# Cosine attention and a quick-GELU layer: the issue order of all engines taken from an earliest-due-first plan, and the softmax denominators of three head pairs stored together

## The chip, the core and the metric

The kernel runs on one core of a Trainium2 chip. Its engines work at the same time, each through its own instructions in the order in which the program gives them: TensorE (PE) multiplies matrices, VectorE (DVE), ScalarE (ACT) and GpSimd (POOL) work on elements, and SyncE (SP) issues most transfers (DMA); POOL issues those of the weights. An instruction waits until what it reads is there and the buffer that it writes is free, and what stands behind it on its engine waits too. The metric is the device time of one execution in microseconds.

## The reference, cut to what matters

```
q_n = q / (norm(q) + 1e-06);  k_n = k / (norm(k) + 1e-06)     # 8 batches, 12 heads, 448 rows, 64 columns
attn = softmax(q_n @ k_n.T / tau)                             # tau = 0.1
x = (attn @ v), heads side by side                            # 3584 x 768
h = x @ w_in                                                  # 768 x 2048
out = (h * (1 / (1 + exp(-1.702 * h)))) @ w_out               # 3584 x 768, float32
```

## The kernel before

The work is cut into 48 **head pairs** x (6 of each batch b). A pair goes through these steps: the loads of q, k and v (`load_qk`, `load_v`, SP, 224 KB each); the squares (`square`, ACT) and their sums (`reduce`, DVE); the inverse norms of a group of pairs (`norm`, ten small DVE instructions); q and k times the norms (`scale`, POOL) and v cast to fp16 (`cast_v`, POOL); the transposes (`transposes`, PE, 8 small matmuls into `tps`, which DVE copies to `qkT`); four chunks of scores (`scores`, PE, into `sp`) and their exponentials (`exp`, ACT); and two attention products (`attend`, PE, into `avp`, one for each head of the pair), which DVE moves to `av`. A row of `av` holds the softmax denominators. Three pairs make a **group** g: its denominators go to DRAM (`den_out`), come back spread over the partitions (`den_in`), are inverted (`den_rcp`, DVE), stored, and come back spread to all partitions as `rcb`; then `normalise` (DVE) makes `xT` from `av` and `rcb`.

When the six `xT` of a batch are there, the layer of that batch can run: 16 blocks of `mm1` (6 matmuls each, line 278, then a tanh on ACT and `gT` on DVE) and then 6 or 8 blocks of `mm2` (16 matmuls each, line 318, then `ost` on ACT and the store of the output).

The order is written out by hand. A loop takes two steps s to a pair. In each step it issues two chunks of scores with their exponentials and one attention product of the pair before, and then the jobs that `at(s, ...)` has put down for that step, half of them and then the other half. Between these `fill` takes matmuls from the queue of the layer, until the share of a step is used up; the share is the work that is left over the steps that are left. Every job stands at a fixed step: the loads at `sq_step` less five, `normalise` five or three steps after the last pair of its group, the first layer block of a batch two steps behind that. The weights are asked for by POOL, `w_in` in four pieces at steps 3, 5, 7 and 9, `w_out` at steps 11 to 17.

Buffers that matter: six for each of q and k, four for v, three `sq`, three `qks`, two `qkT`, two `sp`, eight exponentials, six `av` (one for each pair), three `mm` in PSUM, and one in PSUM that `tps` and `avp` share.

## Time and profile before

| | us |
|---|---|
| median of 3 runs (556.71 to 561.02) | 559.64 |
| the profiled execution, its own time | 559.58 |
| its span, from the first instruction to the last | 557.8 |
| PE busy in the span | 474.8 |
| ACT busy | 310.5 |
| DVE busy | 303.2 |
| POOL busy | 140.7 |

The profile has a page and views that ask the trace. The page cuts the span into 40 equal slices (a digit is the busy share in tenths). Stretches give the busy time of each engine between two times. The waits say for which instruction an engine stood idle, how long in total, how many times, and the longest. The timeline lists instructions by their start, with the idle time before them in brackets and what ended it. All times are in us from the first instruction, durations called "mean" are in ns.

### The profile page before, as it was taken

The page shows a single profiled execution, that of the slowest core. Times are in us where ns is not written, and L with a number is a line of the kernel's source. Part 1 is how long each engine was busy: PE and PEld are TensorE (multiplying, and loading weights), DVE is VectorE, ACT ScalarE, POOL GpSimd, SP SyncE. Part 2 cuts the span into 40 slices and gives each one's busy share as a digit, 9 for nine tenths or more (in the row PEclk, how much of TensorE's full clock was granted, in tenths as well). Part 3 has the DMA queues.
Part 4 walks back from the last instruction along what each step waited for, and adds up shares of the span by engine and source line. Part 5 has one row for each costly group of instructions (what it writes and reads, how often), then busy time and mean ns, then how long its engine had stood idle before and what let it go on. Part 6 is the DMA issues. An engine that isn't in the chain of part 4 may idle for free.

```text
span 557.8 us, 7958 instructions
## 1 busy us (share of the span) xinstructions
PE 474.8 (85%) x2816; PEld 236.2 (42%) x2816; DVE 303.2 (54%) x677; ACT 310.5 (56%) x473; POOL 140.7 (25%) x205
## 2 busy tenths in 40 slices
PE   0665617699989999999889998999799999996996
PEld 0222202244544554445344554455344554452553
DVE  6456355667267645675476636764676525532510
ACT  3745707277557655775757656765667445621421
POOL 2370624320403232322323050323232320000000
PEclk9997758699999999999999999999899999997999
DMA  8568979621531436132613343143502220002012
GB/s 237 159 124 179 177 171 175 142 84 58 146 100 51 124 108 181 49 93 80 181 50 110 96 130 116 52 121 108 152 18 60 64 82 29 26 30 82 1 28 86
DMA packets 55431, 56.61 MB, mean 101 GB/s; under 512 B 8064, under 2 KB 51936, under 8 KB 55392
## 3 DMA queue, kind: packets, MB, share of 16 engines
q1 hardware_dynamic: 50144, 49.82, 31.8%
q0 software_dynamic: 5248, 6.29, 7.0%
q8 instruction: 22, 0.36, 0.3%
q14 instruction: 17, 0.14, 0.1%
HBM read 51.20 MB, written 11.18 MB: 112 GB/s over the span
## 4 chain that ended last, share of the span: by engine, by line
PE 65%; DVE 18%; DMA 10%; issue 2%; ACT 2%; SPq 2%; DVEq 0%; ACTq 0%
PE mm L318 23%; PE mm L278 21%; PE avp L213 12%; PE sp L191 8%; DVE xT L263 4%; DVE av L221 3%; DVE n L114 3%; DMA rcp<-rcg 3%; DMA rcb<-rcp 3%; DVE qkT L180 2%; DMA v<-in_v_dram 2%; DVE gT L288 2%; PE tps L174 2%; ACT th L287 2%; DMA q<-in_q_dram 1%
## 5 line engine op out<-in xcount | busy, mean ns | idle before, releaser
L203 ACT ACTIVATE expT<-sp 112x896 f16<-112x896 f32 x192 | 170.3, 914 | 80.6 <-PE sp L191 79.7
L278 PE MATMUL mm<-xT,w_in 128*128 128x448 f16 x768 | 170.2, 362 | 18.6 <-DVE xT L263 18.6
L318 PE MATMUL mm<-w_out,gT 128*128 128x384 f16 x896 | 160.8, 327 | 0.0
L221 DVE TENSOR_SCALAR av<-avp 65x448 f16<-65x448 f32 x96 | 59.5, 620 | 115.1 <-PE avp L213 111.5
L288 DVE SCALAR_TENSOR_TENSOR gT<-th,mm 128x448 f16<-128x448 f16 x128 | 79.0, 620 | 78.0 <-ACT th L287 76.1
L287 ACT ACTIVATE th<-mm 128x448 f16<-128x448 f32 x128 | 69.5, 543 | 88.3 <-PE mm L278 86.7
L318 PEld LDWEIGHTS <-gT 128*128 128x128 f16 x896 | 84.0, 98 | 65.6 <-issue 11.5
L278 PEld LDWEIGHTS <-w_in 128*128 128x128 f16 x768 | 72.4, 99 | 86.8 <-issue 29.5
L156 POOL TENSOR_TENSOR qks<-k,y 112x512 f16<-112x512 f32 x48 | 50.5, 1053 | 188.4 <-DVE y L147 170.8
L213 PE MATMUL avp<-expT,vt 112*128 112x448 f16 x384 | 97.3, 379 | 0.0
L191 PE MATMUL sp<-qkT 64*112 64x448 f16 x384 | 64.2, 411 | 28.6 <-DVE qkT L180 25.5
L167 POOL CAST vt<-v 112x256 f16<-112x256 f32 x96 | 37.2, 401 | 130.8 <-PE avp L213 124.7
L114 DVE TENSOR_REDUCE n<-sq 112x8 f32<-112x512 f32 x96 | 63.9, 676 | 6.0 <-ACT sq L108 5.4
L326 ACT ACTIVATE ost<-mm 128x384 f32<-128x384 f32 x56 | 27.4, 490 | 65.9 <-PE mm L318 63.1
L174 PE MATMUL tps<-ident,qks 112*128 112x112 f16 x384 | 28.9, 223 | 31.1 <-DVE av L221 21.1
L213 PEld LDWEIGHTS <-vt 112*128 112x128 f16 x384 | 36.8, 102 | 43.8 <-issue 16.9
L156 POOL TENSOR_TENSOR qks<-q,y 112x512 f16<-112x512 f32 x47 | 49.2, 1048 | 0.0
L174 PEld LDWEIGHTS <-qks 112*128 112x128 f16 x384 | 25.3, 103 | 54.0 <-issue 39.3
L191 PEld LDWEIGHTS <-qkT 64*112 64x112 f16 x384 | 19.5, 135 | 66.3 <-DVE qkT L180 38.8
L263 DVE TENSOR_TENSOR xT<-av,rcb 64x448 f16<-64x448 f16 x96 | 39.3, 409 | 14.7 <-DMA rcb<-rcp 13.1
L108 ACT ACTIVATE sq<-k 112x512 f32<-112x512 f32 x48 | 30.3, 632 | 6.7 <-DMA k<-in_k_dram 5.2
L180 DVE COPY qkT<-tps 128x896 f16<-128x896 f16 x48 | 29.6, 618 | 5.7 <-PE tps L174 5.4
(23 smaller groups left out, 87.4 us busy)
## 6 DMA issues: line engine op xcount, KB each, us to landing
q<-in_q_dram SPq DMA_DIRECT2D x48, 224.0 KB
k<-in_k_dram SPq DMA_DIRECT2D x48, 224.0 KB
v<-in_v_dram SPq DMA_DIRECT2D x48, 224.0 KB
rcb<-rcp SPq DMA_DIRECT2D x32, 168.0 KB
w_in<-in_moe_w_in_dram POOLq DMA_DIRECT2D x4, 768.0 KB, 10.7
w_out<-in_moe_w_out_dram POOLq DMA_DIRECT2D x4, 768.0 KB, 10.1
out_dram<-ost SPq DMA_DIRECT2D x7, 336.0 KB
out_dram<-ost SPq DMA_DIRECT2D x8, 288.0 KB
```

The costliest lines, as they stand in the source:

```text
L114: nc.vector.tensor_reduce(out=n2s[grp][:, x - grp[0], ti], in_=sqs.pop((x, ti)), axis=AX.X, op=ALU.add,)
L156: (eng or nc.gpsimd).tensor_tensor(out=qkss[x][:, ti].rearrange("p c j d -> p j c d"), in0=src, in1=rss[x][:, ti, :, :, None].to_broadcast ...
L174: nc.tensor.transpose(out=tps[:, ti, c * P : (c + 1) * P], in_=qks[:, ti, c].rearrange("p j d -> p (j d)"), identity=ident[:P, :P],)
L191: nc.tensor.matmul(out=sp[:, j, :S], lhsT=qkT[64 * j : 64 * (j + 1), 1, c * P : (c + 1) * P], rhs=qkT[64 * j : 64 * (j + 1), 0, :], start= ...
L203: nc.scalar.activation(out=e, in_=sps.pop((x, c))[:, :, :S], func=AF.Exp, scale=inv_tau, **kw)
L213: nc.tensor.matmul(out=ps, lhsT=vts[x % 4][:, c, j], rhs=exps[x, c][:, j], start=(c == 0), stop=(c == C - 1),)
L221: nc.vector.tensor_scalar(out=avs[x][:n, j], in0=ps[:n], scalar1=AV_SCALE, scalar2=None, op0=ALU.mult)
L263: nc.vector.tensor_tensor(out=xT[r], in0=av[r, j], in1=rcbs[x // GRP][r, x % GRP], op=ALU.mult)
L278: nc.tensor.matmul(out=ps[:, :S], lhsT=w_in_sb[:, kk, 128 * m : 128 * (m + 1)], rhs=xTs[b, kk], start=(kk == 0), stop=(kk == KT1 - 1),)
L287: nc.scalar.activation(out=th, in_=ps[:, :S], func=AF.Tanh, scale=0.851)
L288: nc.vector.scalar_tensor_tensor(out=gT[:, m], in0=th, scalar=1.0, in1=ps[:, :S], op0=ALU.add, op1=ALU.mult,)
L318: nc.tensor.matmul(out=ps[:, :NW], lhsT=gT[:, kk, 128 * t : 128 * (t + 1)], rhs=w_out_sb[:, kk, cols], start=(kk == 0), stop=(kk == KT2 - 1),)
```

## The change

A class `Plan` replaces the loop over steps, `at`, `fill` and the streams. Every operation is put down with its engine, a duration, a due step, what it comes after, and the buffers that it takes and gives back as counted slots. `order` then runs a clock over that model: an engine that is idle takes, of what is ready and finds its slots free, the operation that is due first. Transfers move one after the other in the queue of their issuer at 270 KB per us (half of that while the other issuer's queue is busy) and land 1.9 us later. The instructions are issued in the order in which the operations start in the model; the engines themselves still wait for data and buffers, not for the model's times.

Due steps are two to a pair as before; the layer of a batch is due from five steps after its last pair on (`LAG`). Some operations are cut apart so that each stands on one engine: the copy out of PSUM from the matmuls, the tanh and the gate from `mm1`, `norm` in two halves, a `mm2` block in four parts of four matmuls. The k load of a pair stands ahead of its q load.

`av` is one tile for three pairs, in two buffers, where each pair had one of six. So the denominators of a group leave in two stores (one for each j, three rows of 448) where there were six of one row: 32 stores in place of 96. No matmul, activation or load is added or removed.

```diff
-MM1_NS = 189
-MM2_NS = 163
...
+SEM_US = 0.1
+SWITCH_US = 0.12
+DMA_US = 1.9
+DMA_BYTES_PER_US = 270e3
...
+class Plan:
...
+    def order(self):
...
+        while len(out) < len(ops):
+            for e in idle:
+                held = []
+                while idle[e] <= now and ready[e]:
+                    due, i = heapq.heappop(ready[e])
+                    _, us, _, emit, _, takes, _, nbytes, rows = ops[i]
+                    if any(self.free[s] < k for s, k in takes):
+                        held.append((due, i))
+                        continue
+                    for s, k in takes:
+                        self.free[s] -= k
+                    out.append((now, i, emit))
+                    if e == "PE" and rows != mode:
+                        mode = rows
+                        us += SWITCH_US
+                    idle[e] = end = now + us
+                    if nbytes is not None:
+                        share = 2 if any(t > end for q, t in dma.items() if q != e) else 1
+                        dma[e] = max(dma.get(e, 0.0), end) + share * nbytes / DMA_BYTES_PER_US
+                        end = dma[e] + DMA_US
+                    heapq.heappush(events, (idle[e], i, True))
+                    heapq.heappush(events, (end + SEM_US, i, False))
...
+            now = events[0][0]
+            while events and events[0][0] <= now:
+                _, i, own = heapq.heappop(events)
+                if not own:
+                    for s, k in ops[i][6]:
+                        self.free[s] += k
...
-    p_av = pool("p_av", 6)
+    p_av = pool("p_av", 2)
...
-            avs[x] = p_av.tile([128, 2, S], FP16, name="av")
...
+    def attended(x, j):
+        if j == 0 and x % GRP == 0:
+            av = p_av.tile([128, GRP, 2, S], FP16, name="av")
+            for i in range(GRP):
+                avs[x + i] = av[:, i]
+            avgs[x // GRP] = av
...
-    def den_out(x, j):
...
-        nc.sync.dma_start(out=dens[x // GRP][r : r + 1, :], in_=avs[x][row : row + 1, j])
...
+    def den_out(g, j):
+        if j == 0:
+            dens[g] = dram.tile([2, GRP, S], FP16, name="den")
...
+        nc.sync.dma_start(out=dens[g][j : j + 1], in_=avgs[g][row : row + 1, :, j])
...
+    plan = Plan(
+        dict(q=6, k=6, v=4, sq=3, qks=3, vt=4, qkT=2, sp=2, a=1, exp=8, av=6)
+        | dict(x=2 * HP, mm=3, th=3, g=1, ost=3)
+    )
...
+    LAG = 5
...
+            add(("sq", ti, x), "ACT", 0.53, early - 2 + ti * 0.1, partial(square, x, ti),
+                after=[("load", nm, x)], takes=[("sq", 1)])
...
+        add(("tp", x), "PE", 0.45, s - 1, partial(transposes, x),
+            after=[("scale", 0, x), ("scale", 1, x)], takes=[("a", 1), ("qkT", 1)], frees=[("qks", 2)])
...
+        add(("x", x), "DVE", 0.75, 2 * (g + 1) * GRP + 3, partial(normalise, x), after=rin,
+            takes=[("x", 1)], frees=[("av", 1)])
...
+            add(("mm1", b, m), "PE", 1.134, due, partial(mm1, b, m), after=after,
+                takes=[("mm", 1)], frees=[("x", HP * (m == KT2 - 1))])
...
-        at(3 + 2 * i, load_w_in, i)
-        at(11 + 2 * i, load_w_out, i)
...
+        add(("w_in", i), "POOL", 1.0, 3 + 2 * i, partial(load_w_in, i), after=[("cast", i)], nbytes=1.57e6)
+        add(("w_out", i), "POOL", 1.0, 11 + 2 * i, partial(load_w_out, i), after=[("w_in", 3)], nbytes=1.57e6)
...
-    for s in range(min(later), max(max(later), 2 * NPAIR + 2) + 1):
...
-            scores(x, half)
...
+    for _, _, emit in plan.order():
+        emit()
```

Three places show how instructions move. The first is POOL at the start of the program: `CAST vt` is the cast of v (x2 for the two heads), `qks` the scaling, `DMA w_in` a piece of the weights. Before:

```order
L156 TENSOR_TENSOR qks<-k_122,y_187 112x2x4x64
L167 CAST vt_116<-v_132 112x4x64 x2
L156 TENSOR_TENSOR qks<-k_126,y_213 112x2x4x64
L156 TENSOR_TENSOR qks<-q_124,y_213 112x2x4x64
L167 CAST vt_117<-v_138 112x4x64 x2
L156 TENSOR_TENSOR qks<-k_130,y_213 112x2x4x64
L156 TENSOR_TENSOR qks<-q_128,y_213 112x2x4x64
L167 CAST vt_118<-v_144 112x4x64 x2
L156 TENSOR_TENSOR qks<-k_136,y_341 112x2x4x64
L156 TENSOR_TENSOR qks<-q_134,y_341 112x2x4x64
L167 CAST vt_119<-v_150 112x4x64 x2
L357 DMA w_in<-in_moe_w_in_dram 128x6x512
```

And with the change:

```order
L238 CAST vt_116<-v_148 112x4x64 x2
L420 DMA w_in<-in_moe_w_in_dram 128x6x512
L227 TENSOR_TENSOR qks<-k_140,y_171 112x2x4x64
L238 CAST vt_117<-v_156 112x4x64 x2
L420 DMA w_in<-in_moe_w_in_dram 128x6x512
L238 CAST vt_118<-v_167 112x4x64 x2
L420 DMA w_in<-in_moe_w_in_dram 128x6x512
L227 TENSOR_TENSOR qks<-k_144,y_215 112x2x4x64
L227 TENSOR_TENSOR qks<-q_146,y_215 112x2x4x64
L227 TENSOR_TENSOR qks<-k_150,y_215 112x2x4x64
L227 TENSOR_TENSOR qks<-q_152,y_215 112x2x4x64
L238 CAST vt_119<-v_189 112x4x64 x2
```

The first three pieces of `w_in` now stand behind the casts of pairs 0, 1 and 2, and the fourth follows the last row shown; before, the first piece stood behind the cast of pair 3. The four pieces of `w_out` now stand together behind the scaling of pair 10's k; before, one stood behind each of the casts of pairs 7 to 10.

The second place is SP around the denominators of the first group of pairs (0 to 2). `den` is the store of denominators, `dnm` the load that brings them back, `rcp` the store of their inverses, `rcb` the load that spreads these. Before, from the fifth of the group's six stores on:

```order
L233 DMA den_313<-av_460 1x448
L101 DMA v32_474<-in_v_dram 112x2x256
L93 DMA q32_476<-in_q_dram 112x2x256
L93 DMA k32_478<-in_k_dram 112x2x256
L233 DMA den_313<-av_460 1x448
L240 DMA dnm_514<-den_313 112x24
L93 DMA q32_521<-in_q_dram 112x2x256
L93 DMA k32_523<-in_k_dram 112x2x256
L233 DMA den_547<-av_536 1x448
L101 DMA v32_549<-in_v_dram 112x2x256
L247 DMA rcp_584<-rcg_582 112x24
L250 DMA rcb_586<-rcp_584 64x3x448 x2
```

With the change, from the rows behind that group's two stores on:

```order
L164 DMA k32_536<-in_k_dram 112x2x256
L164 DMA q32_541<-in_q_dram 112x2x256
L317 DMA dnm_573<-den_483 112x24
L164 DMA v32_585<-in_v_dram 112x2x256
L164 DMA k32_596<-in_k_dram 112x2x256
L164 DMA q32_599<-in_q_dram 112x2x256
L327 DMA rcp_648<-rcg_635 112x24
L164 DMA v32_668<-in_v_dram 112x2x256
L164 DMA k32_677<-in_k_dram 112x2x256
L164 DMA q32_681<-in_q_dram 112x2x256
L310 DMA den_689<-av_578 3x1x448 x2
L332 DMA rcb_709<-rcp_648 64x1344 x2
```

The stores of single pairs are gone from between the loads. Ahead of the first `den` stand 28 loads (22 before), ahead of the first group's `rcb` 37 (35 before), and ahead of the second group's 43 (44 before). The `rcb` of the first group stands behind the `den` of the second.

The third place is DVE where the first `xT` are made. `av_691` is the output of pair 5, `av_357` the tile of pairs 0 to 2, `av_810` that of pairs 6 to 8; `n2_3` are sums of squares; the first `qkT` of each excerpt is pair 6's before and pair 8's now. Before:

```order
L180 COPY qkT_669<-tps_660 128x896
L221 TENSOR_SCALAR av_691<-avp_692 65x448
L114 TENSOR_REDUCE n2_3_632<-sq_653 112x8
L114 TENSOR_REDUCE n2_3_632<-sq_655 112x8
L263 TENSOR_TENSOR xT0_704<-av_302,rcb_586 64x448 x2
L263 TENSOR_TENSOR xT1_707<-av_381,rcb_586 64x448 x2
L221 TENSOR_SCALAR av_691<-avp_723 128x448
```

With the change:

```order
L254 COPY qkT_760<-tps_729 128x896
L177 TENSOR_REDUCE n2_3_793<-sq_782 112x8
L177 TENSOR_REDUCE n2_3_793<-sq_791 112x8
L343 TENSOR_TENSOR xT0_800<-av_357,rcb_709 64x448 x2
L343 TENSOR_TENSOR xT1_803<-av_357,rcb_709 64x448 x2
L343 TENSOR_TENSOR xT2_807<-av_357,rcb_709 64x448 x2
L299 TENSOR_SCALAR av_810<-avp_769 65x448
L299 TENSOR_SCALAR av_810<-avp_813 128x448
```

Before, the first two pairs' `xT` stood between the two halves of pair 5's `av`, and pair 7's `qkT` behind them. Now the `qkT` of pairs 7 and 8 stand ahead of all three pairs' `xT`, and the two halves of pair 6's `av` behind.

## Rows read from the trace of the kernel before

**Rows 1.** The page: busy us (share of the span) and instructions; then PE's busy tenths in 40 slices.

```profile
PE 474.8 (85%) x2816; PEld 236.2 (42%) x2816; DVE 303.2 (54%) x677; ACT 310.5 (56%) x473; POOL 140.7 (25%) x205
...
PE   0665617699989999999889998999799999996996
```

**Rows 2.** Stretches: length, busy (instructions) by engine, PE clock, DMA share, GB/s.

```profile
10.00:98.00 88.00, 49.08 (x233) 19.19 (x234) 47.49 (x115) 46.80 (x66) 37.57 (x55) 0.83 0.80 170
...
106.00:506.00 400.00, 381.24 (x2352) 193.66 (x2351) 230.62 (x495) 244.84 (x375) 98.00 (x140) 0.99 0.31 89
```

**Rows 3.** Waits of PE from 0 to 98: us in total, times, longest.

```profile
PE sp L191 <- DVE qkT L180: 20.6, 10, 5.1
PE tps L174 <- DVE av L221: 16.6, 8, 9.3
PE tps L174 <- POOL qks L156: 10.1, 1, 10.1
```

**Rows 4.** Timeline, 60 to 106: start, us, engine, line, out<-in, count, [idle before <-releaser].

```profile
60.71 0.55 PE L174 MATMUL tps<-ident,qks 112*128 112x112 f16 x8 [0.71 <-DVE av L221]
...
65.76 0.63 ACT L108 ACTIVATE sq<-k 112x512 f32<-112x512 f32 x1 [0.65 <-DVE n L114]
...
66.30 1.70 ACT L203 ACTIVATE expT<-sp 112x896 f16<-112x896 f32 x2
...
71.85 0.38 DVE L263 TENSOR_TENSOR xT<-av,rcb 64x448 f16<-64x448 f16 x1 [5.53 <-DMA rcb<-rcp]
...
74.21 1.19 DVE L263 TENSOR_TENSOR xT<-av,rcb 64x448 f16<-64x448 f16 x3 [1.97 <-DMA rcb<-rcp]
...
75.43 0.62 DVE L221 TENSOR_SCALAR av<-avp 128x448 f16<-128x448 f32 x1
76.08 1.28 DVE L114 TENSOR_REDUCE n<-sq 112x8 f32<-112x512 f32 x2
76.10 0.90 PE L174 MATMUL tps<-ident,qks 112*128 112x112 f16 x8 [9.26 <-DVE av L221]
...
78.02 0.24 SPq L233 DMA_DIRECT2D den<-av  x1
...
80.10 1.03 POOL L156 TENSOR_TENSOR qks<-k,y 112x512 f16<-112x512 f32 x1 [13.28 <-DVE y L147]
...
105.17 0.53 PE L278 MATMUL mm<-xT,w_in 128*128 128x448 f16 x1 [1.53 <-DVE xT L263]
```

**Rows 5.** DMA queues: packets, MB, share of 16 engines; first 0 to 14, then 28 to 60.

```profile
q1 hardware_dynamic: 3456, 3.31, 86.8%
...
q0 software_dynamic: 2383, 2.39, 47.7%
q1 hardware_dynamic: 2538, 2.30, 25.6%
```

**Rows 6.** The weights' issue: ns min/median/max, first and last start.

```profile
L357 POOL DMA_DIRECT2D w_in<-in_moe_w_in_dram x4: 882/883/1009, 31.6 to 57.1; - x4
```

**Rows 7.** Waits of PE from 106 to 506.

```profile
PE mm L278 <- DVE xT L263: 8.0, 8, 1.7
PE sp L191 <- DVE qkT L180: 4.9, 14, 0.8
PE tps L174 <- DVE av L221: 4.4, 7, 0.7
PE sp L191 <- ACT expT L203: 0.8, 2, 0.4
```

**Rows 8.** Waits of PE from 506 to 514.

```profile
PE mm L278 <- DVE xT L263: 5.3, 3, 4.7
```

**Rows 9.** Timeline around the last batch's layer.

```profile
495.99 3.58 PE L318 MATMUL mm<-w_out,gT 128*128 128x384 f16 x21
...
500.17 5.85 PE L318 MATMUL mm<-w_out,gT 128*128 128x384 f16 x35
...
510.81 2.06 DVE L263 TENSOR_TENSOR xT<-av,rcb 64x448 f16<-64x448 f16 x5 [0.72 <-DMA rcb<-rcp]
```

More of the change, by code (lines that the diff above doesn't have):

```diff
@@ L298, in store, with mm1, tanh @@
-    def store(b2, t, ost, cols):
+    gts, mms, ths, osts = {}, {}, {}, {}
+    def mm1(b, m):
+        ps = mms[b, m] = ps_m.tile([128, 512], FP32, name="mm")
+        for kk in range(KT1):
+            nc.tensor.matmul(
+                out=ps[:, :S],
+                lhsT=w_in_sb[:, kk, 128 * m : 128 * (m + 1)],
+                rhs=xTs[b, kk],
+                start=(kk == 0),
+                stop=(kk == KT1 - 1),
+            )
+    def tanh(b, m):
+        ths[b, m] = p_th.tile([128, S], FP16, name="th")
+        nc.scalar.activation(
+            out=ths[b, m], in_=mms[b, m][:, :S], func=AF.Tanh, scale=0.851
+        )
@@ new lines, in gate, with mm2 @@
+    def gate(b, m):
+        if b % 2 == 0 and m == 0:
+            gts[b // 2] = p_g.tile([128, KT2, 2 * S], FP16, name="gT")
+        nc.vector.scalar_tensor_tensor(
+            out=gts[b // 2][:, m, (b % 2) * S : (b % 2 + 1) * S],
+            in0=ths.pop((b, m)),
+            scalar=1.0,
+            in1=mms.pop((b, m))[:, :S],
+            op0=ALU.add,
+            op1=ALU.mult,
+        )
+    def mm2(b2, t, n, part):
+        if part == 0:
+            mms[b2, t, n] = ps_m.tile([128, 512], FP32, name="mm")
+        for kk in range(4 * part, 4 * part + 4):
+            nc.tensor.matmul(
+                out=mms[b2, t, n][:, :NW],
+                lhsT=gts[b2][:, kk, 128 * t : 128 * (t + 1)],
+                rhs=w_out_sb[:, kk, NW * n : NW * (n + 1)],
+                start=(kk == 0),
+                stop=(kk == KT2 - 1),
+            )
@@ new lines @@
+        if x == grp[0]:
+            reds = [("red", ti, y) for y in grp for ti in range(2)]
+            add(("norm", 0, grp), "DVE", 0.9, early, partial(norm_a, grp), after=reds)
+            add(("norm", 1, grp), "DVE", 1.3, early, partial(norm_b, grp), after=[("norm", 0, grp)])
+        add(("load", "v", x), "SP", 0.5, s - 9, partial(load, x, v32, v, "v32"),
+            after=[("s", x - 4, 0)] if x >= 4 else [], takes=[("v", 1)], nbytes=PAIR_BYTES)
+        add(("cast", x), "POOL", 0.75, s - 1, partial(cast_v, x), after=[("load", "v", x)],
+            takes=[("vt", 1)], frees=[("v", 1)])
@@ new lines @@
+        add(("tp", x), "PE", 0.45, s - 1, partial(transposes, x),
+            after=[("scale", 0, x), ("scale", 1, x)], takes=[("a", 1), ("qkT", 1)], frees=[("qks", 2)])
+        add(("qkT", x), "DVE", 0.53, s - 1, partial(transposed, x), after=[("tp", x)],
+            frees=[("a", 1)])
+        for c in range(C):
+            add(("s", x, c), "PE", 0.19, s + c // 2, partial(scores, x, c), after=[("qkT", x)],
+                takes=[("sp", 1)], frees=[("qkT", int(c == C - 1))], rows=64)
+            add(("exp", x, c), "ACT", 0.83, s + c // 2 + 0.1, partial(exp, x, c),
+                after=[("s", x, c)], takes=[("exp", 1)], frees=[("sp", 1)])
@@ new lines @@
+        for j in range(2):
+            es = [("exp", x, c) for c in range(C)] + [("cast", x)]
+            if j == 1:
+                es.append(("av", x, 0))
+            add(("at", x, j), "PE", 0.757, s + 2 + j, partial(attend, x, j), after=es,
+                takes=[("a", 1)], frees=[("exp", 4 * j), ("vt", j)])
+            add(("av", x, j), "DVE", 0.54, s + 2 + j, partial(attended, x, j), after=[("at", x, j)],
+                takes=[("av", 1 - j)], frees=[("a", 1)])
+            if x % GRP == GRP - 1:
+                add(("den", g, j), "SP", 0.45, s + 2 + j, partial(den_out, g, j),
+                    after=[("av", y, j) for y in range(x - GRP + 1, x + 1)], nbytes=3e3)
```

332 lines of the change are left out of this document (155 added, 177 removed).

## The prediction

> **What bounds the kernel now.** I read the page first. PE is the busiest engine, 474.8 of 557.8 us, and its slices fall into three parts: a thin start of about 100 us, a dense middle, and a dip near the end [rows 1]. So I asked for the stretches and for PE's waits in each.
>
> In the middle, 106 to 506, PE is busy for 381.24 of 400 us [rows 2]: it is the bound there, and no order can give back more than the 18.8 us that it stands idle. The waits name 18.1 of these: for `xT` 8.0, for `qkT` 4.9, for `av` 4.4, for exponentials 0.8 [rows 7].
>
> In the start nothing is dense. From 10 to 98 PE is busy for 49 of 88 us, the transfers take 0.80 of their engines, and ACT, DVE and POOL about half of their time [rows 2]. PE waits 47.3 us there, for `qkT` (20.6), `av` (16.6) and `qks` (10.1) [rows 3]. The timeline shows how the longest comes about. DVE stands at an `xT` that waits for `rcb`, 5.53 us and again 1.97; the second half of pair 5's `av`, whose product is long done, stands behind it and starts at 75.43; so `tps`, which needs that buffer of PSUM, starts at 76.10 after 9.26 us. The last denominator store of batch 0 goes at 78.02, and the sixth matmul of the first layer block, which needs the last `xT` of that batch, at 105.17 [rows 4]. From there on PE has work at all times, so **the start is worth what that matmul moves**, since in both orders nine and a half pairs of attention stand ahead of it.
>
> Near the end PE waits 5.3 us for the last batch's `xT` [rows 8]. After that everything depends on one batch's layer, which the change leaves alone.
>
> The profiled execution took 559.58 us, 1.8 over its span and the same as the median of 559.64. The sum is made against 559.6.
>
> **Term 1, the start.** The transfers first. Alone, 3.31 MB of loads took 86.8% of 14 us, and in the mixed stretch ten loads (2.30 MB) took 25.6% of 32 us, so a load costs 0.82 us of all 16 engines. There 2.39 MB of weights (three pieces of 0.786 MB) took 47.7%, so a piece costs 5.0 us [rows 5]. The transposes of pair 6 were the first that the old order held up for long; they started at 60.71 [rows 4]. They need the norms of pairs 6 to 8, so the 25th load in SP's new order, and by then all four pieces of `w_in` have been asked for as well. That is 25 x 0.82 + 4 x 5.0 = 40.5 us of transfers: 40.5 us if the engines never rest, 50.6 at the 0.80 of now. From the sums of squares (76.08) to the scaling (80.10, and 1.03 for each of k and q) take 6.1 us more [rows 4]. So these transposes start between 47 and 57; I take 52.
>
> The second products of pair 5 come one pair's step later. ACT sets that step: four exponentials (1.70 for two) and two squares (0.63 each) are 4.7 us [rows 4]. Then comes the chain from `den` to the first block. It took 27.2 us at the start of this kernel (78.02 to 105.17) [rows 4]. Near the end, with nothing ahead in the queue, it took from the last product (matmuls go on at 500.17) to the end of the last `xT` at 512.87, that is 12.7 us [rows 9]. The new order sends one store for three pairs, without waits between the loads, but three loads still stand between each two of its steps, so I take 23, nearer the upper end. 52 + 4.7 + 23 is 80 for the matmul that is at 105.17 now: **minus 25**. The bounds: 57 + 4.7 + 27.2 = 89, minus 16. On the other side the chain ends at 64, but ACT's four pairs (6 to 9, 18.8 us behind 47, and the scores of a tenth) do not: 70, minus 35.
>
> By the Trainium skill's page "DMA: Bandwidth & Descriptors", section "Queues, rings and completion order", each transfer engine takes turns between the queues that have work, packet by packet. By that rule the loads keep half of the engines while `w_in` is under way, and the sum would be 11 us lower (505; the second rival works it out from rows). The trace agrees in the mixed stretch as far as bytes go, 2.30 and 2.39 MB [rows 5].
>
> What the start pays for this: POOL does a cast and an issue of 0.88 us [rows 6] ahead of the first scaling, so the first transposes come up to 1.7 us later. I cost that at nothing, since the transposes of pair 6 wait for transfers; without that cover it is 1.7. The two more copies `qkT` ahead of the first `xT` on DVE are work that PE can use while `rcb` is under way; that is where the 9.26 us went. Next to be late are pair 6's two `av`, which stand behind all three pairs' `xT`; behind them wait `rcg` of the second group and the `qkT` of pair 9. That lies inside the 23 us. `w_out` is asked for in one go behind the scaling of pair 10's k; its four pieces are 20 us of transfers, and the first `mm2` stands behind all 16 blocks of a batch's `mm1`, so I cost them at nothing; if they came 5 us late, it is 5.
>
> **Term 2, the middle.** Of 18.1 us I expect 14 back. The waits for `xT` (8.0 in eight) come from `normalise` standing at a fixed step, right at the first block that needs it. Now the block is issued only when the plan has the six `xT`, and half a block of `mm2` and a pair of score chunks more stand between the last product of a batch and its first layer block. The waits for `av` (4.4) are those of `tps` behind a product: between them stood one block of `mm1`, and now mostly a pair of score chunks and one block. The `qkT` waits shrink for the same reason: a product stands between transposes and scores. The bounds: nothing (each wait replaced by another of its size) and 18.8 (all idle time of the stretch). New waits can come where a product now follows the transposes after a single block of `mm1` and needs the PSUM buffer that the copy `qkT` must empty first; I leave 4 us for these. **Minus 14.** The 64 stores fewer (0.24 us of SP each) are off PE's path.
>
> **Term 3, the end.** Behind the last product stand 64 matmuls of `mm2` where 32 stood. 21 of them take 3.58 us [rows 9], so 32 more cover 5.4 us of a wait of 5.3 [rows 8]. The chain itself is no shorter than its transfers. I take **minus 4.6**; the bounds are 0 (the chain grows as much) and 5.3.
>
> **The sum:** 559.6 - 25 - 14 - 4.6 = **516**.
>
> **Rivals.**
> - *The weights hold the loads back.* `w_in` was asked for at 31.6 to 57.1 [rows 6], and now three pieces stand among the first POOL rows. If the loads get the worse share, pair 6 starts no earlier than 60.7 and the chain keeps its 27.2: 60.7 + 4.7 + 27.2 = 92.6, minus 12.6. The time is 528. For it: 0.80 is already high. Against: 20.5 us of loads and 20 of weights fit into 60 with room.
> - *The loads keep half.* In the mixed stretch the two queues moved the same bytes. If the first seven loads run alone (5.7 us) and the next 18 at half pace (29.5), the norms follow at 35 with `w_in` unfinished, and pair 6 starts at 41: 41 + 4.7 + 23 = 69, minus 36. The time is 505. Against: `w_in` itself took more than its half there, 47.7% to 25.6% [rows 5].
> - *The middle swaps its waits.* In a fixed line an operation that the plan has too early stops its engine; then term 2 is nothing, 530. For it: each of ACT and DVE is busy for 0.6 of the middle, in order. Against: the new order keeps the blocks' buffers and the spacing.
> - *Nothing is gained:* a new wait of the start's size, 20 us, takes the place of the old ones, and the middle swaps its waits: 559.6 - 5 = 555.
> - *Slower: the tile of three pairs.* The first `av` of group g+2 must now wait for all three `xT` of group g, where one sufficed, and `av`, `qkT` and gates queue behind it on DVE. This is the 9.26 us of rows 4, if it came back at each group. It must eat 43.6 us and 5.6 more; over the 14 groups with a predecessor that is 3.5 us a group. At 4 us it is 572. Against it: in the middle a group of three pairs lasts 30 us (400 us hold 13.3 groups) and the chain 12.7 to 27.2, and no wait for `av` there exceeds 0.7 [rows 7].
>
> **How the numbers follow.** The forecast 0.48 (508 to 527), the weights first 0.15, loads at half 0.10, the middle's waits swapped 0.15, nothing gained 0.07, slower 0.05. The range from 502 to 538 holds the first four, less a little at each edge, and goes no further. A measurement of this kernel can tell about 1%, 5.6 us, from no change: faster 0.88, within it 0.07, slower 0.05.
>
> **What would show it.** Term 1: the sixth matmul of the first layer block near 80, pair 6's transposes near 52, `w_in` issued between about 8 and 25. Term 2: waits for `xT` in the middle under 2 us in all, PE busy over 0.97. Term 3: the wait ahead of the last batch's layer under 1.5 us. It is wrong if the first layer block starts after 95, if PE waits for `av` or `qkT` by more than 10 us in the middle, or if a new wait of DVE for `rcb` appears at every group.

## The result, and the profile after

The changed kernel takes **514.22 us** (median of 4 runs, 512.71 to 516.54) where the kernel before takes 560.33 (median of 4): a ratio of 0.9187, 95% interval 0.9123 to 0.9251. The forecast was 516, between 502 and 538. The profiled execution took 516.54 us with a span of 514.7, against 559.58 and 557.8: 43.0 us less, where the sum of the prediction had 43.6. It is the slowest of the four runs of the changed kernel; by the medians the gain is 46.1 us. The stretches below are those of the profiled executions.

The total is nearly the one forecast, but its parts are not. Here is the span of both kernels cut at the same three places: the sixth matmul of the first layer block, the first matmul of the last batch's layer, and the sixth matmul there. First the kernel before (length, then busy time and instructions of PE, PEld, DVE, ACT, POOL, PE clock, DMA share, GB/s; PEld is the loading of weights into PE, PE clock the granted share of full speed):

```profile
0.00:105.17 105.17, 50.84 (x237) 19.65 (x238) 60.34 (x160) 52.34 (x73) 42.74 (x65) 0.83 0.80 176
105.17:505.86 400.69, 381.92 (x2356) 194.16 (x2356) 230.62 (x495) 245.10 (x375) 98.00 (x140) 0.99 0.31 89
505.86:512.92 7.06, 1.79 (x6) 0.50 (x5) 2.31 (x6) 0.49 (x1) 0.00 (x0) 0.81 0.34 104
512.92:557.80 44.88, 40.22 (x219) 21.91 (x218) 9.94 (x16) 12.61 (x24) 0.00 (x0) 0.95 0.13 36
```

And the changed kernel:

```profile
0.00:90.78 90.78, 56.24 (x255) 22.61 (x256) 60.80 (x162) 55.14 (x75) 42.38 (x65) 0.76 0.89 202
90.78:466.29 375.51, 373.53 (x2339) 192.54 (x2337) 232.37 (x494) 241.72 (x373) 100.57 (x140) 0.99 0.34 96
466.29:471.10 4.81, 1.61 (x6) 0.49 (x5) 2.32 (x6) 0.49 (x1) 0.00 (x0) 0.89 0.51 151
471.10:514.75 43.65, 39.30 (x219) 21.66 (x218) 9.94 (x16) 12.63 (x24) 0.00 (x0) 0.97 0.13 37
```

The start shrank by 14.4 us, the middle by 25.2, the stretch with the wait near the end by 2.25, and the last layer by 1.2. The prediction had 25, 14 and 4.6 for the first three. It took the same work to stand ahead of the first cut in both orders, but in the changed kernel 18 more matmuls do (255 for 237), worth 1.7 us at the rate of the middle (8 transposes of 49 ns, 6 score matmuls of 97, 4 product matmuls of 189), so on equal work it gained 16.1 and the middle 23.5.

The page's slices, to be set against [rows 1] (PE's busy share and granted clock in tenths, 40 slices of 12.9 us):

```profile
PE   0677767998999999999999999999999999997996
...
PEclk9986656899999999999999999999999999998999
```

The dense part now begins at the eighth slice and has no thin digit before the end. PE's waits in it, to be set against [rows 7]:

```profile
PE tps L245 <- DVE av L299: 0.8, 1, 0.8
PE avp L282 <- DVE qkT L254: 0.7, 1, 0.7
```

1.5 us instead of 18.1, and none for `xT`; DVE waits for `rcb` 0.4 us ahead of the last group. What the prediction wanted to see of term 2 is there: PE is busy for 373.53 of 375.51 us.

**The start.** The `w_in` pieces are issued at 8.98, 12.17, 13.79 and 19.49 (31.6 to 57.1 in [rows 6]). Pair 6's transposes start at 52.09, as forecast (52). The timeline shows what they stood behind (start, us, engine, line, operation; in brackets the idle time before and what ended it):

```profile
42.00 0.21 DVE L218 TENSOR_TENSOR y<-y,t 112x48 f32<-112x48 f32 x1
...
42.34 1.04 POOL L227 TENSOR_TENSOR qks<-k,y 112x512 f16<-112x512 f32 x1 [3.93 <-issue]
...
43.34 1.04 POOL L227 TENSOR_TENSOR qks<-q,y 112x512 f16<-112x512 f32 x1
...
47.20 1.65 PE L282 MATMUL avp<-expT,vt 112*128 112x448 f16 x4 [0.71 <-DVE av L299]
...
49.70 1.68 PE L282 MATMUL avp<-expT,vt 112*128 112x448 f16 x4
...
51.42 0.62 DVE L299 TENSOR_SCALAR av<-avp 128x448 f16<-128x448 f32 x1 [1.32 <-PE avp L282]
...
52.09 0.91 PE L245 MATMUL tps<-ident,qks 112*128 112x112 f16 x8 [0.71 <-DVE av L299]
```

The norms are out at 42.2 and k and q of pair 6 are scaled by 44.4. What stands between this and 52 is a chain of PE and DVE over the one PSUM buffer that `avp` and `tps` share: a product, its `av`, the next product, each round 2.4 us, because four matmuls of a product take 1.65 us there where they take 0.92 at 27.39 or in the middle. The first layer block comes 10.8 us later than forecast:

```profile
66.30 2.38 DVE L343 TENSOR_TENSOR xT<-av,rcb 64x448 f16<-64x448 f16 x6
...
71.13 0.62 DVE L299 TENSOR_SCALAR av<-avp 128x448 f16<-128x448 f32 x1 [1.74 <-PE avp L282]
...
72.39 0.29 DVE L322 RECIPROCAL rcg<-dnm 112x24 f16<-112x24 f16 x1
...
77.61 1.12 SPq L332 DMA_DIRECT2D rcb<-rcp  x2
...
85.40 0.62 DVE L254 COPY qkT<-tps 128x896 f16<-128x896 f16 x1
...
85.94 3.10 DVE L343 TENSOR_TENSOR xT<-av,rcb 64x448 f16<-64x448 f16 x6
...
88.94 2.42 PE L354 MATMUL mm<-xT,w_in 128*128 128x448 f16 x6
```

`rcg` of the second group, whose data were asked for at 61.82, runs at 72.39 behind the three pairs' `xT` and two halves of `av`, though the last packet of that load had moved at 65.0; `xT` of pairs 3 to 5 run at 85.94 without waiting for anything, right behind the `qkT` of pair 10.

**The end**, to be set against [rows 8, 9]:

```profile
460.22 0.30 DVE L322 RECIPROCAL rcg<-dnm 112x24 f16<-112x24 f16 x1 [3.50 <-DMA dnm<-den]
...
461.80 0.79 SPq L412 DMA_DIRECT2D out_dram<-ost  x2
462.69 0.37 SPq L327 DMA_DIRECT2D rcp<-rcg  x1
...
464.89 1.14 SPq L332 DMA_DIRECT2D rcb<-rcp  x2
...
468.57 2.48 DVE L343 TENSOR_TENSOR xT<-av,rcb 64x448 f16<-64x448 f16 x6 [8.05 <-DMA rcb<-rcp]
469.43 0.35 PE L354 MATMUL mm<-xT,w_in 128*128 128x448 f16 x1 [2.41 <-DVE xT L343]
```

64 matmuls now stand behind the last product (35 before, [rows 9]), but the chain to the last `xT` (471.05) takes 15.0 us from the last product's end (456.05), where it took 12.5 (500.33 to 512.87). `rcp` was issued at 462.69, though `rcg` had ended at 460.52: on SP two stores of the output stood ahead of it, waiting for their `ost` at 461.29. PE waited 3.2 us.

### The profile page after: what moved, and what is told of

The parts are those of the page before. It is cut to its first block, busy times and chain, and to the rows that moved or that the text cites. A ratio compares the mean times of both kernels' runs of the same rounds, so it can differ in the third digit from the quotient of the medians.

```text
span 514.7 us, 7833 instructions
## 1 busy us (share of the span) xinstructions
PE 470.7 (91%) x2816; PEld 237.3 (46%) x2816; DVE 305.4 (59%) x677; ACT 310.0 (60%) x473; POOL 143.0 (28%) x205
## 4 chain that ended last, share of the span: by engine, by line
PE 75%; DVE 9%; DMA 1%; ACT 1%; issue 1%; SPq 0%; DVEq 0%; ACTq 0%
PE mm L384 27%; PE mm L354 25%; PE avp L282 12%; PE sp L263 7%; PE tps L245 3%; DVE xT L343 3%; DVE gT L371 2%; DVE av L299 1%; DVE qkT L254 1%; DVE n L177 1%; DMA rcb<-rcp 1%; DMA rcp<-rcg 0%; ACT expT L274 0%; DVE t L203 0%; DVE t L206 0%
## 5 line engine op out<-in xcount | busy, mean ns | idle before, releaser
L274 ACT ACTIVATE expT<-sp 112x896 f16<-112x896 f32 x192 | 166.1, 915 | 68.5 <-PE sp L263 62.6
L354 PE MATMUL mm<-xT,w_in 128*128 128x448 f16 x768 | 159.9, 359 | 3.2 <-DVE xT L343 3.2
L384 PE MATMUL mm<-w_out,gT 128*128 128x384 f16 x896 | 155.4, 326 | 0.0
L238 POOL CAST vt<-v 112x256 f16<-112x256 f32 x96 | 40.6, 425 | 268.5 <-PE avp L282 256.1
L384 PEld LDWEIGHTS <-gT 128*128 128x128 f16 x896 | 83.8, 98 | 63.7 <-issue 12.5
L282 PE MATMUL avp<-expT,vt 112*128 112x448 f16 x384 | 98.9, 384 | 12.6 <-DVE qkT L254 6.2
L282 PEld LDWEIGHTS <-vt 112*128 112x128 f16 x384 | 38.6, 103 | 56.0 <-issue 29.4
L227 POOL TENSOR_TENSOR qks<-k,y 112x512 f16<-112x512 f32 x48 | 50.0, 1043 | 12.5 <-issue 7.0
L343 DVE TENSOR_TENSOR xT<-av,rcb 64x448 f16<-64x448 f16 x96 | 38.8, 404 | 10.1 <-DMA rcb<-rcp 8.5
```

Of the source, the lines that this page charges most:

```text
L227: (eng or nc.gpsimd).tensor_tensor(out=qkss[x][:, ti].rearrange("p c j d -> p j c d"), in0=src, in1=rss[x][:, ti, :, :, None].to_broadcast ...
L274: nc.scalar.activation(out=e, in_=sps.pop((x, c))[:, :, :S], func=AF.Exp, scale=inv_tau, **kw)
L282: nc.tensor.matmul(out=ps, lhsT=vts[x % 4][:, c, j], rhs=exps[x, c][:, j], start=(c == 0), stop=(c == C - 1),)
L343: nc.vector.tensor_tensor(out=xT[r], in0=av[r, j], in1=rcbs[x // GRP][r, x % GRP], op=ALU.mult)
L354: nc.tensor.matmul(out=ps[:, :S], lhsT=w_in_sb[:, kk, 128 * m : 128 * (m + 1)], rhs=xTs[b, kk], start=(kk == 0), stop=(kk == KT1 - 1),)
L384: nc.tensor.matmul(out=mms[b2, t, n][:, :NW], lhsT=gts[b2][:, kk, 128 * t : 128 * (t + 1)], rhs=w_out_sb[:, kk, NW * n : NW * (n + 1)], st ...
```

## The experiments

All of these ran with the kernel before beside them; a ratio is that to the kernel before. The last four columns are the same four stretches of each profiled execution, by the start of the matmuls.

| kernel | median us | ratio (95%) | start | middle | wait | last layer |
|---|---|---|---|---|---|---|
| before | 560.33 | | 105.2 | 400.7 | 7.1 | 44.9 |
| changed | 514.22 | 0.9187 (0.9123 to 0.9251) | 90.8 | 375.5 | 4.8 | 43.6 |
| e1_pair_stores | 515.26 | 0.9183 (0.9137 to 0.9229) | 90.0 | 374.9 | 4.6 | 45.1 |
| e2_before_triple | 556.64 | 0.9926 (0.9898 to 0.9954) | 104.4 | 399.9 | 7.0 | 44.6 |
| e3_w_in_late | 516.79 | 0.9213 (0.9186 to 0.9241) | 92.6 | 373.4 | 4.6 | 45.1 |
| e4_w_out_early | 517.27 | 0.9224 (0.9195 to 0.9252) | 92.3 | 375.8 | 4.4 | 42.5 |
| e5_spin | 510.03 | 0.9081 (0.9063 to 0.9100) | 85.5 | 374.2 | 4.6 | 43.9 |
| e5b_spin_more | 520.02 | 0.9256 (0.9236 to 0.9277) | 93.0 | 374.6 | 6.3 | 44.8 |
| e6_no_latency | 593.74 | 1.0575 (1.0534 to 1.0616) | 83.2 | 463.9 | 1.5 | 42.5 |
| e7_tail | 511.42 | 0.9089 (0.9063 to 0.9116) | 90.2 | 375.3 | 1.7 | 42.5 |
| f1_spin_tail | 504.83 | 0.9017 (0.9000 to 0.9034) | 84.1 | 374.2 | 2.1 | 42.5 |
| f2_start | 504.16 | 0.9003 (0.8984 to 0.9023) | 82.3 | 376.1 | 2.0 | 42.5 |
| g1_latency_3 | 527.14 | 0.9418 (0.9394 to 0.9443) | 87.3 | 384.7 | 7.8 | 44.0 |
| g2_latency_14 | 508.48 | 0.9056 (0.9023 to 0.9089) | 78.1 | 383.2 | 2.5 | 42.5 |

### Which part of the change carries the gain

The first undoes the denominators of three pairs in one store, and keeps the plan:

```diff
-    p_av = pool("p_av", 2)
+    p_av = pool("p_av", 6)
...
-            if x % GRP == GRP - 1:
-                add(("den", g, j), "SP", 0.45, s + 2 + j, partial(den_out, g, j),
-                    after=[("av", y, j) for y in range(x - GRP + 1, x + 1)], nbytes=3e3)
+            add(("den", x, j), "SP", 0.45, s + 2 + j, partial(den_out, x, j),
+                after=[("av", x, j)], nbytes=1e3)
```

> The changed kernel with one part undone: the planned order stays, but each pair has its own `av` tile again (six buffers) and each denominator row its own store (96 instead of 32). Theory: the order carries the whole gain, the stores stood on SP beside its other work; 512 to 517 us, the sixth matmul of the first layer block within 1.5 us of 90.8. Rival 1, the stores between the loads cost the start: that matmul after 94 and 519 us or more. Rival 2, the shared tile holds back `av` of the group after next: 510 us or less.

515.26 us, the sixth matmul at 89.98: as the theory had it. The second puts that part alone into the kernel before:

```diff
-    p_av = pool("p_av", 6)
+    p_av = pool("p_av", 2)
...
-        for j in range(2):
-            at(2 * (x + 1) + j, den_out, x, j)
+        for j in range(2 if x % GRP == GRP - 1 else 0):
+            at(2 * (x + 1) + j, den_out, x // GRP, j)
```

> The kernel before with the other part alone: `av` as one tile for three pairs in two buffers, two stores of three rows for a group instead of six of one row, the hand-written order unchanged. Theory: no change, 556 to 563 us, the sixth matmul of the first layer block at 103 to 107, since the old waits come from the fixed steps. Rival 1, fewer stores make the chain from the denominators to `xT` shorter: that matmul before 101, 554 us or less. Rival 2, the shared tile makes the first `av` of a group wait for all three `xT` of the group before last: waits of PE for `av` in the middle above 10 us (4.4 before), 565 us or more.

556.64 us, a ratio of 0.9926 (0.9898 to 0.9954): inside the theory's bounds, at their lower edge; a gain of 3.5 us by the medians is clear of noise, but no single stretch holds it. Its waits in the middle are those of before, 7.8 for `xT`, 4.9 for `qkT`, 4.5 for `av`. So the shared tile does no harm (the rival on the slower side has no footing in either kernel), and the plan's order carries nearly all of the 46 us.

### What set the start: the transfers?

`w_in` later, near its old place:

```diff
-        add(("w_in", i), "POOL", 1.0, 3 + 2 * i, partial(load_w_in, i), after=[("cast", i)], nbytes=1.57e6)
+        add(("w_in", i), "POOL", 1.0, 3 + 2 * i, partial(load_w_in, i), after=[("cast", i + 3)], nbytes=1.57e6)
```

> The changed kernel with the four pieces of `w_in` behind the casts of pairs 3 to 6 instead of 0 to 3, near where the kernel before had them. Theory: the weights' place is worth little, because the first layer block hangs on the second group's chain and not on the loads: the transposes of pair 6 come 2 to 6 us earlier than 52.1, the sixth matmul of the first block stays within 3 us of 90.8, 513 to 518 us. Rival 1, weights first hold the loads back: that matmul before 87 and 510 us or less. Rival 2, asking for the weights early is what gained in the start: that matmul after 95, 519 us or more.

516.79 us and 92.6. The scaling of pair 6's k began at 41.36, 1.0 us earlier, but its transposes started at 51.86, 0.2 us earlier and not 2 to 6: the transfers did not set them. The time is as the theory had it. How the queues shared the engines can be read in the changed kernel, from 20 to 36 us, when loads and weights were both waiting (packets, MB, share of 16 engines):

```profile
q0 software_dynamic: 1999, 2.01, 73.8%
q1 hardware_dynamic: 2003, 1.91, 44.0%
```

The two moved the same number of packets to two in a thousand. So the loads did keep half of the packets, as the second rival had it, and an early pair 6 was possible (scaled by 44.4); the time did not follow, since the products stood in between. The Trainium skill's page "DMA: Bandwidth & Descriptors", section "Queues, rings and completion order", says that an engine takes turns between queues packet by packet. The trace agrees with that.

`w_out` earlier, into the stretch where no transfer moves:

```diff
-        add(("w_out", i), "POOL", 1.0, 11 + 2 * i, partial(load_w_out, i), after=[("w_in", 3)], nbytes=1.57e6)
+        add(("w_out", i), "POOL", 1.0, 8, partial(load_w_out, i), after=[("s", 5, 0)], nbytes=1.57e6)
```

> The changed kernel with the four pieces of `w_out` asked for behind the first scores of pair 5 (about 40 us) instead of at 65.7 to 68.7, so that they move while the transfers stand at zero (43 to 53 us) and are gone when the second group's denominators come round. Theory 1: `w_out` stands in the way of `rcp` and `rcb` of the second group (`rcb` is issued 4.9 us behind `rcp`): that step falls under 3 us, the sixth matmul of the first block comes at 86 to 89, 510 to 513 us. Theory 2: DVE's line (the reciprocal of the second group and its `xT` behind `av`, sums of squares and `qkT`) sets that matmul: within 1.5 us of 90.8, 513 to 516 us. Theory 3: the loads of pairs 9 to 11 are held back instead: the matmul after 92.5, 516 us or more.

517.27 us. The first half of theory 1 came true: `rcb` of the second group was issued 1.4 us behind `rcp` instead of 4.9.

```profile
73.19 0.32 SPq L327 DMA_DIRECT2D rcp<-rcg  x1
...
74.60 1.12 SPq L332 DMA_DIRECT2D rcb<-rcp  x2
...
87.24 3.25 DVE L343 TENSOR_TENSOR xT<-av,rcb 64x448 f16<-64x448 f16 x6
```

But `xT` stood at its place in DVE's line, behind the `qkT` of pair 10 and the norms of pairs 12 to 14, and started without a wait at 87.24, later than in the changed kernel (85.94); the sixth matmul came at 92.3, the edge of what theory 2 allowed. The time lies in theory 3's range, but pairs 7 and 8 were transposed 1.7 and 1.6 us earlier than in the changed kernel and pair 9 only 0.5 us later, so held-back loads of pairs 9 to 11 do not explain it. Of the 1.5 us, 0.5 stand at the sums of pair 12, ahead of the first `xT`: they waited 4.08 us for their squares, 2.02 in the changed kernel. Data that come 3 us earlier are worth nothing to an instruction whose place is fixed.

### What set the start: PE's clock

From 43.3 to 57.0 and from 60.4 to 84.3 the granted clock of the changed kernel is 0.50 (the lower of its two levels, 1.2 GHz), after a stretch of scores and transposes with waits of 0.2 to 1.1 us between them. This run fills the waits with matmuls that nobody reads:

```diff
+    def spin(n):
+        ps = ps_m.tile([128, 512], FP32, name="mm")
+        for _ in range(n):
+            nc.tensor.matmul(out=ps[:, :S], lhsT=ident, rhs=zero, start=True, stop=True)
...
         tpss[x] = tps
+        if x <= 10:
+            spin(4)
...
         avps[x, j] = ps
+        if x <= 9:
+            spin(3)
```

> The changed kernel with idle matmuls in the start: zeros times the identity, 448 columns, into a PSUM buffer of the layer that nobody reads, 4 behind each of the first 11 groups of transposes and 3 behind each of the first 20 attention products; the output is that of the changed kernel. The product that takes 0.76 us in the middle takes 1.65 us from 42 to 57 and from 60 to 88, at a granted clock of 0.50. Theory: PE's level there comes from the waits between its matmuls; with them filled the clock stays near 1.0 in most of 42 to 88, products take 0.76 us, the sixth matmul of the first layer block comes at 80 to 87 instead of 90.8, 505 to 511 us. Rival 1: the second group's chain of denominators and DVE set that matmul: clock higher, but the matmul within 1.5 us of 90.8, 513 to 516 us. Rival 2: the clock stays at 0.50 and the extra matmuls come on top: after 93, 517 us or more.

510.03 us, the sixth matmul at 85.5: as the theory had it. Its start as a stretch (columns as above), and two rows of its timeline:

```profile
0.00:85.49 85.49, 61.64 (x356) 28.02 (x357) 61.04 (x162) 54.04 (x74) 42.27 (x65) 0.96 0.92 214
```

```profile
66.41 1.65 PE L290 MATMUL avp<-expT,vt 112*128 112x448 f16 x4 [4.11 <-DVE av L309]
...
76.78 0.93 PE L290 MATMUL avp<-expT,vt 112*128 112x448 f16 x4
```

There are 101 matmuls more ahead of the cut, and it comes 5.3 us sooner: the clock is 0.96 instead of 0.76, and a product takes 0.93 us. Only behind the wait of 4.11 us is it 1.65 again (the clock is 0.50 from 64.2 to 71.1).

> As the run before, with 8 idle matmuls behind each of the first 11 groups of transposes and 5 behind each of the first 20 products, 0.95 us at the rate of the middle, so more than the 0.72 us for which PE waits for the copy out of PSUM. Theory: the waits are filled wholly, the clock is near 1.0 from 20 on, and the sixth matmul comes within 2 us of that of the run with fewer, at 80 to 87; 505 to 512 us. Rival 1 (the chain sets it): 513 to 517 us. Rival 2 (the extra matmuls only take PE's time): 518 us or more.

With 8 and 5 instead of 4 and 3 the clock is 0.98, as the theory had it, but the cut comes at 93.0 and the time is 520.02, which is rival 2's. 82 matmuls more than in the run above stand ahead of the cut, 15.5 us of PE at 189 ns each, and the cut comes 7.5 us later: what the waits no longer hold comes on top.

### What set the middle

```diff
-SEM_US = 0.1
+SEM_US = 0.0
...
-DMA_US = 1.9
+DMA_US = 0.0
```

> The changed kernel whose plan reckons with no landing time of a transfer (0 instead of 1.9 us) and no delay of a signal (0 instead of 0.1 us); nothing else is changed, and the engines still wait for the data. Theory: the middle gained because the plan knows when `xT` will be there; now layer blocks and `xT` stand too early again: PE waits for `xT` by 6 us or more between the first layer block and the last batch (0 in the changed kernel, 8.0 before), and the first block, which the plan now puts behind the first product of pair 6, waits for its `xT` while products stand behind it: 522 to 540 us. Rival: due steps, slots and spacing gave the middle, the latencies little: waits for `xT` under 3 us, 517 us or less.

593.74 us, 33 more than the kernel before. The direction was the theory's, the size and the place were not: PE does not wait for `xT` at all in the middle. DVE does. From 92 to 537 (engine, what it waits for, us in total, times, longest), DVE and then PE:

```profile
DVE xT L343 <- DMA rcb<-rcp: 48.5, 24, 4.9
...
DVE rcg L322 <- DMA dnm<-den: 31.7, 13, 3.4
```

```profile
PE tps L245 <- DVE av L299: 22.7, 10, 5.1
PE avp L282 <- DVE qkT L254: 20.9, 14, 2.1
PE mm L354 <- DVE gT L371: 16.4, 6, 3.7
```

DVE stands 80.2 us at `rcb` and `dnm`, 6.2 us for each of 13 groups, and `av`, `qkT` and gates stand behind it. That is the mechanism that the prediction named as its rival on the slower side, with another cause; there it decided from 3.5 us a group on.

> The changed kernel whose plan reckons with 3.0 us from the end of a transfer to its landing instead of 1.9. With 0 the time was 593.7 us: DVE stood 48.5 us at `xT` for `rcb` and 31.7 us at the reciprocals for `dnm`, some 6 us for each group. Theory: only a plan that has a transfer too early stops DVE; one that has it 1.1 us too late spaces the same work further and costs little: no wait of DVE for `rcb` or `dnm` above 1 us in the middle, 512 to 520 us. Rival: the plan is as sensitive on this side, since operations stand too late in a fixed line: 525 us or more.

With 3.0 us the time is 527.14, as the rival had it. DVE hardly stops: from 92 us to the last group it waits 2.8 us for `rcb` and `dnm`, where it was 0.4 in the changed kernel and 80.2 with a landing time of 0. But PE is busy for 375.82 of 384.65 us of the middle where it was 373.53 of 375.51, and the stretch with the wait near the end is 7.8 us long (4.8).

> The changed kernel whose plan reckons with a landing time of 1.4 us instead of 1.9. In the last group of the changed kernel, where SP and DVE only wait for the transfers, the small ones landed 1.2 to 1.9 us behind the end of their issue (den 1.25, dnm 1.2, rcp 1.8). Theory 1: what counts is whether the plan is earlier than the chip, step by step; at 1.4 that is so for `rcp` and `rcb` alone, by half a us each: waits of DVE for `rcb` and `dnm` of 5 to 20 us in the middle over some 14 groups (80.2 with 0, 12.0 with 1.9, most of these two near the end), 516 to 526 us. Theory 2: the loss goes with the missing time, 0.5 of 1.9 of 79 us: waits of 25 us and more, 531 to 540 us. Rival: the chosen order matters more than the landing time (as with 3.0, where 12.9 us were lost without waits of DVE): waits under 15 us and yet 527 us or more, most of it in the start, where the plan now puts the first layer block ahead of the products of pair 8.

With 1.4 us the time is 508.48, **less than any of the three theories allowed**. DVE's waits for `rcb` and `dnm` are 6.1 us from 92 us to the last group, as theory 1 had it, and the middle takes 7.7 us more, for 4.0 us more work in it. The gain is in the start, and 3.4 us of it in the last two stretches. With this number the plan happens to put the second group's `rcg` ahead of pair 6's `av`, and that group's `xT` ahead of pair 9's `qkT`:

```profile
60.81 2.53 DVE L343 TENSOR_TENSOR xT<-av,rcb 64x448 f16<-64x448 f16 x6
63.38 0.30 DVE L322 RECIPROCAL rcg<-dnm 112x24 f16<-112x24 f16 x1
...
74.43 0.66 DVE L343 TENSOR_TENSOR xT<-av,rcb 64x448 f16<-64x448 f16 x1 [1.39 <-DMA rcb<-rcp]
76.03 2.02 DVE L343 TENSOR_TENSOR xT<-av,rcb 64x448 f16<-64x448 f16 x5 [0.94 <-DMA rcb<-rcp]
```

`rcg` at 63.38 instead of 72.39, the sixth matmul at 78.1 instead of 90.8 (with 34 matmuls less ahead of it, 4.0 us). So the landing time acts in two ways. At 0 DVE stops at each group. At 1.4, 1.9 and 3.0 it stops for 6.1, 0.4 and 2.8 us, and the time still moves by some 19 us with the order that happens to fall out. Which number is best these points do not say, nor how much of the changed kernel's own gain is such a chance.

### The end, and the sum of what was found

```diff
-                            after=[("ost", b2, t, n)], frees=[("ost", int(n == 1 and i == len(segs) - 1))],
+                            after=[("ost", b2, t, n)] + ([("rin", 15, 1)] if b == 6 and t else []),
+                            frees=[("ost", int(n == 1 and i == len(segs) - 1))],
```

> The changed kernel with two output stores of one tile moved behind the last group's two `rcb` in SP's order; they stood between `dnm` and `rcp`, and `rcp` was issued at 462.69, 2.2 us after its reciprocal had ended. Theory: SP's line made the last chain longer than before (15.0 us from the last product to the last `xT`, 12.5 in the kernel before): PE's wait ahead of the last batch's layer falls from 3.2 us to under 1.5, 511.5 to 513.5 us. Rival: the transfers themselves are slower beside the output's stores, the wait stays above 2.5 us, 514 to 516 us.

511.42 us, PE's wait 0.5: as the theory had it (its range began at 511.5).

```profile
459.48 0.30 DVE L322 RECIPROCAL rcg<-dnm 112x24 f16<-112x24 f16 x1 [3.60 <-DMA dnm<-den]
459.81 0.31 SPq L327 DMA_DIRECT2D rcp<-rcg  x1
...
461.19 1.14 SPq L332 DMA_DIRECT2D rcb<-rcp  x2
```

`rcp` is now issued 0.03 us behind `rcg`. The last layer, too, is 1.2 us shorter (42.5 for 43.6). In the table it is 42.5 wherever the stretch with the wait is at most 2.5 us, and anything from 42.5 to 45.1 where that is longer: a long wait can leave PE at the lower clock, and need not. In the changed kernel the granted clock is 0.50 from 470.0 to 473.4, in e1_pair_stores from 467.9 to 474.8, and in e4_w_out_early, with a stretch of 4.4 us, it stays at 1.00.

> The idle matmuls of the start (4 behind transposes, 3 behind products) and the two output stores moved behind the last `rcb`, together. Theory: the two act in different places and add up, 4.2 and 2.8 us below 514.2: 506 to 508.5 us. Rival: the shorter wait near the end was due in part to the state of PE after the slower start, and they overlap: 509 to 511 us.

504.83 us, below the 506 to 508.5 expected. By the medians the two together gave 2.4 us more than the sum of the two; by the spans of the profiled executions (514.7, 508.1, 509.7 and 502.9) they add up, 6.6 and 5.0 against 11.8. They act in different places. Its runs lie within 504.65 to 505.76, those of the changed kernel within 512.71 to 516.54. The last step adds two orders on DVE:

```diff
-                after=[("sq", ti, x)], frees=[("sq", 1)])
+                after=[("sq", ti, x)] + ([("x", 2)] if x == 12 else []), frees=[("sq", 1)])
...
-            add(("norm", 0, grp), "DVE", 0.9, early, partial(norm_a, grp), after=reds)
+            add(("norm", 0, grp), "DVE", 0.9, early, partial(norm_a, grp), after=reds + ([("x", 5)] if x == 12 else []))
```

> The run with both, and two orders on DVE in the start in addition: the sums of squares of pair 12 stand behind the first group's `xT` (they waited 2.1 us for their squares ahead of them), and the norms of pairs 12 to 14 behind the second group's `xT`. Theory: what is left of the missed 10 us in the start is DVE's line; the second group's reciprocal comes 2 to 4 us earlier than 69.4 and the sixth matmul of the first layer block 2 to 4 us earlier than in the run with both: 503 to 506 us. Rival: the transfers of the second group or the products of pairs 7 to 9 set that matmul: within 1 us of the run with both, 506 to 508.5 us.

The sixth matmul comes at 82.3, 1.8 us sooner than in the run with both, but the middle takes 1.9 us more, and 504.16 us cannot be told from 504.83. It lies in the theory's range only because the run with both came out lower than expected; that these orders change nothing in the time is what the rival said. Both beat the changed kernel by some 10 us; that is a ratio of 0.900 to the kernel before.

## Why the prediction was right in its total, and not in its terms

**Right:** that the start and the waits of the middle were where the time lay, that the layer of a batch issued by a plan ends the waits for `xT` (8.0 to 0), the use of three-pair stores (no part in it), `w_in` early as no danger to the loads, and the total, 43.6 forecast and 43.0 measured in the profiled executions (46.1 by the medians). That it is so near is luck: two errors of some 10 us cancel.

**Term 1, forecast minus 25, measured minus 14.4** (16.1 on equal work): outside its bounds (minus 16 to 35) as it stands, at their small end on equal work. The first step held as a number and not as a mechanism: the 40.5 us of transfers are there (the fourth `w_in` piece landed at 39.9, the norms were out at 42.2), but then the products set pair 6's transposes and not the 6.1 us from squares to scaling. The step that failed is the chain from `den` to the first block, taken at 23 us, with 27.2 as its upper bound: from the second `den` (58.21) to the sixth matmul (90.78) it took 32.6. The prediction had put `rcg`'s wait behind `xT` and `av` "inside the 23 us"; that alone held `rcg` from 65.0 to 72.39. Shown by runs: with the waits filled (clock 0.96) the cut comes at 85.5; under the plan for 1.4 us, which has `rcg` ahead of `av`, at 78.1 (82.1 on equal work). That plan differs in more than this, so what the place of `rcg` is worth alone is not shown. Not weighed at all was the clock, which [rows 2] show as well, 0.83 from 10 to 98; the estimate of 4.7 us for a pair's step took ACT's pace, and at 0.50 one of the pair's two products takes 2.4 with its `av`. The prediction also set the 47.3 us of PE's waits against the stretch from 10 to 98, in which PE idles for only 38.9; [rows 3] begin at 0, and the 10.1 us for `qks` lie ahead of the first matmul. No term rests on that.

**Term 2, forecast minus 14 with 18.8 as the most, measured minus 25.2** (23.5 on equal work). "No order can give back more than the 18.8 us that it stands idle" is the sentence that failed. Idle time is not all that a wait costs. This is one wait for `xT` of the kernel before:

```profile
397.96 0.35 PE L278 MATMUL mm<-xT,w_in 128*128 128x448 f16 x1 [0.16 <-DVE xT L263]
400.05 0.35 PE L278 MATMUL mm<-xT,w_in 128*128 128x448 f16 x1 [1.74 <-DVE xT L263]
...
400.63 2.03 PE L278 MATMUL mm<-xT,w_in 128*128 128x448 f16 x6
402.58 0.99 PE L191 MATMUL sp<-qkT 64*112 64x448 f16 x4
```

```profile
398.00:402.00 4.00, 2.27 (x15) 1.15 (x15) 2.92 (x6) 0.93 (x2) 0.00 (x0) 0.88 0.52 145
402.00:406.00 4.00, 4.00 (x17) 1.48 (x16) 0.90 (x3) 2.15 (x4) 0.00 (x0) 0.69 0.00 0
```

The matmuls start 2.09 us apart where 0.19 is their pace: 1.90 are lost for 1.74 of idle, since the first runs to its end instead of overlapping the next. Then the granted clock is at 0.50 from 401.1 to 404.5: six matmuls take 2.03 us (1.13 at their pace), all of it counted as busy. It need not fall: behind a wait of 1.73 us at 280.08 it stayed at 1.00. Over the middle of the kernel before, 36 waits hold 18.8 us idle and lose 23.2 from start to start; in the changed kernel 7 hold 2.0 and lose 3.1. So 16.8 us of idle time came back where 14 were forecast, and with what the waits cost beyond it 20.1 of the 23.5. The clock stood at 0.50 for 9.2 us of the middle before and for 3.8 after; at half speed that is, as an estimate, 2.7 of the other 3.4.

**Term 3, forecast minus 4.6, measured minus 2.25** in the wait and minus 1.2 behind it. The cover was nearly right: 64 matmuls, 10.4 us, but in place of 35 and 5.7 us, not of 32. The sentence "the chain itself is no shorter than its transfers" left out that SP's line can make it longer, by 2.5 us. Moving two stores gave it back (a wait of 0.5).

**The rivals:** the weights did not hold the loads back; the middle did not swap its waits; the shared tile cost nothing; the loads kept half and it did not show in the time.

## What to carry to other kernels

An order made from a modelled pipeline is worth what its landing times are worth on the side of too early: with none the same plan was 80 us slower than with 1.9 us, and slower than the order by hand, because the engine that normalises stood still for each group. Beyond that, look where the plan puts the one short instruction of a long chain (here a reciprocal of 0.3 us, 7.4 us late) and what stands ahead of it on the engine and on the queue. And count a wait of PE at more than its idle time: the last matmul ahead of it runs to its end, and a lower clock behind it can come on top. In a thin stretch a few unread matmuls in the waits can pay.

## What was not expected of the hardware

After waits between matmuls of 0.2 to 1.1 us the granted clock of the changed kernel went to 0.50 at 43.3 us and stayed there for 13.7 us, though PE was busy for 4.29 of 5 us in the stretch from 45 to 50. The waits in that stretch are those for the one PSUM buffer, 0.71 us each. Matmuls in these waits brought the clock of the start from 0.76 to 0.96. The Trainium skill's page "TensorE: Matmul & The Clock Gate", section "A second HAM failure mode: psum-queue depth-cycling", tells of a kernel that cycles through PSUM banks and in which small idle times between groups of matmuls make the clock change back and forth between its two levels. The trace agrees in the fall; back and forth it went less, with 13.7 us at one level.
